# Dealing GpSimd's share of the zero stores to the DMA engines anew, and issuing part of it earlier

## Chip, cores and metric

The kernel runs on one core of one Trainium2 chip. The metric is the device time of one execution in microseconds (us), less is better. Three timed runs gave a median of 272.18 us (272.06 to 272.75). One further execution was recorded by the profiler. TensorE is PE (PEld its weight loads), VectorE DVE, ScalarE ACT, GpSimd POOL and SyncE SP; L302 is line 302 of the kernel before. A queue in which an engine issues its DMAs has a q behind its name (SPq).

## What is computed

The forward is a layer norm, a decode step of grouped-query attention over a sliding window of the cache, a gated feed-forward with GELU, and a residual. The kernel returns its output and the gradients of all inputs for a given `grad_out`. Shapes: batch 4, one token, D = 512, 32 query heads, 8 key/value heads of 128, caches of 4096 positions with a window of the last W = 1024, F = 1792.

```python
def _A_ref(x, k_cache, v_cache, wq, wo):
    q = (x @ wq).reshape(B, Sq, Hq, Dh).transpose(0, 2, 1, 3)
    k = jnp.repeat(k_cache[:, :, Sk - W:, :], rep, axis=1)
    v = jnp.repeat(v_cache[:, :, Sk - W:, :], rep, axis=1)
    scores = jnp.einsum("bhqd,bhkd->bhqk", q, k) * (Dh ** -0.5)
    p = softmax(scores)
    o = jnp.einsum("bhqk,bhkd->bhqd", p, v)
    return o.transpose(0, 2, 1, 3).reshape(B, Sq, Hq * Dh) @ wo

def _B_ref(x, w_gate, w_up, w_down):
    return (gelu(x @ w_gate) * (x @ w_up)) @ w_down

xn = layernorm(x)
out = x + _A_ref(xn, ...) + _B_ref(xn, ...)
# outputs: out, then its gradients to x, k_cache, v_cache, wq, wo, w_gate, w_up, w_down
```

The gradients of the two caches (`out_2`, `out_3`, each 4 x 8 x 4096 x 128 in bf16) are zero in the first K0 = 3072 positions, which lie outside the window. These zeros, 50 MB, are the largest part of what the kernel writes.

## The kernel before

Everything is done once, in stages: layer norm and the feed-forward's forward and backward (matrices `wg_sb`, `wu_sb`, `wd_sb`), the queries (`qr_ps`, `q_ps`), then for each batch entry the attention's forward and backward over the window (tiles `ka`, `kb`, `va`, results through `stg`), at last the weight gradients of `wq` and `wo` (`dw_ps`, tiles `late` and `stg`) and the output rows.

The order of PE, DVE, ACT and POOL instructions is chosen by a scheduler up to the attention loop, from dependences and from the place in the program; there a changed line can move others. SP's order is the written one throughout: it holds all loads and stores but two kinds, and its DMAs run in the order of issue on each DMA engine's queue. An SP instruction that waits holds up all that stand behind it.

**Zeros.** `ztile` (128 partitions of 12288 bytes) is cleared by POOL at L224. A piece is 12288 bytes, 48 positions of one head. `ztodo` lists 32 units, each 2 heads of 64 pieces, 1.5 MB. SP writes 31 of them: `zeros(n)` (L298-307) issues n units, each as one DMA whose source is 64 partitions read twice, and holds each behind the fourth unit before it. `result()` (L114-119) issues as many units ahead of a store as the list `before` says; six more stand behind the loads of `va` and `kb` (L461 and L463: two and four). The 32nd unit (`zog`, `zb`, `zg`: the last of `out_3`) goes by POOL in parts:

```python
    def part_zeros(m0, rows, each, part, after=None):
        z = nc.gpsimd.dma_start(
            out=zog[zb, zg:zg + ZG, 0:K0, :].rearrange("g (m j) d -> m g (j d)", m=ZP)[m0:m0 + rows * each],
            in_=bass.AP(tensor=ztile.tensor, offset=ztile[part:part + 1, :].offset,
                        ap=[[4 * ztile[:].ap[0][0], rows], [0, ZG * each], [1, ZW]]))
```

One call is one DMA: `rows` source partitions (every fourth from `part` on), each read 2 x `each` times. Three calls follow the clearing of `dhs` (L420-424): 3 rows of 10 pieces, 2 rows of 2, 3 rows of 10. A fourth, 8 rows of 8 pieces, stands at the beginning of the last phase (L819) and waits for the last SP unit issued before it.

**The stretch that the prediction walks through** is the feed-forward's backward (L339-391). `a_b` (the product of the two branches) is transposed to `aT` (L346); `aSP`, cleared by POOL at L348, gets four diagonal blocks of `a_b` by four DVE instructions at L350. `wd_sb` is transposed in four parts into `scr` (L94), and 16 matmuls add up `da_ps`; from it DVE makes `dhu` (L373), `ua` (L374, its tile is shown as `stg`) and `dhg` (L375). The 14 matmuls `dwd_ps<-dy_b,aSP` make the gradient of `w_down`; `evac` (L83-92) copies each to `stg` on ACT or DVE, by a running estimate of the load of both. `result()` stores it in two halves, then come the loads of `ka`, and the queries.

Of the kernel before, what the change touches and what calls it, by code (L numbers as in the profile page):

```python
# [19 lines left out]
def kernel(  # L20
# [24 lines left out]
    nc = tc.nc  # L45

    B, Sq, D = A_x.shape
    _, G, Sk, Dh = A_k_cache.shape
# [4 lines left out]
    K0 = Sk - W  # L53
# [29 lines left out]
    def evac(out, in_, n):  # L83

        ca, cd = (190 + n) / 1.2, (130 + n) / 0.96
        eng = "act" if load["act"] + ca <= load["dve"] + cd else "dve"
        load[eng] += ca if eng == "act" else cd
        if eng == "act":
            return nc.scalar.copy(out=out, in_=in_)  # L89
        return nc.vector.tensor_copy(out=out, in_=in_)  # L90

    def t32(out, in_, n):
        load["dve"] += (130 + n) / 0.96
        nc.vector.transpose(out=out, in_=in_)  # L94

    def pairs(ap):
        return ap.bitcast(U32)

    def scratch():
        return scrp.tile([P, 1024], U32, name="scr", tag="scr")  # L100
# [6 lines left out]
    def stg_tile():  # L107

        if not halves:
            pair = stg_pair()  # L110
            halves.extend(pair[:, h] for h in range(2))
        return halves.pop(0)
# [3 lines left out]
    def result(*parts):  # L116
        zeros(min(before.popleft(), len(ztodo)))
        for out, in_ in parts:
            nc.sync.dma_start(out=out, in_=in_)
# [19 lines left out]
    def mm(out, lhsT, rhs, first=True, last=True, pos=None):  # L139
        kw = {} if pos is None else {"tile_position": pos}  # L140
        nc.tensor.matmul(out, lhsT=lhsT, rhs=rhs, start=first, stop=last, **kw)  # L141

    def bank(name, tag="w", shape=(P, 512), dt=FP32):
        pool = {"w": ps_w, "x": ps_x}.get(tag, ps_a)
        return pool.tile(list(shape), dt, name=name, tag=tag)
# [75 lines left out]
    ZP = P // 2  # L221
    ZW = K0 // ZP * Dh
    ztile = const.tile([P, ZW], BF16, name="ztile")
    nc.gpsimd.memset(ztile[:].bitcast(FP32), 0.0)  # L224


    stats = const.tile([P, nc.vector.BN_STATS_DIM], FP32, name="stats")
# [32 lines left out]
    def window(dram, b, h):  # L260

        return dram[b, h * G // 2:(h + 1) * G // 2, K0:Sk, :].rearrange("g (m j) d -> m g (j d)", j=2 * J)

    def alternate(tl, h):

        t_ = tl[h:h + 1]
        return bass.AP(tensor=t_.tensor, offset=t_.offset,
                       ap=[[2 * t_.ap[0][0], P // 2], [2 * J * Dh, G // 2], [1, 2 * J * Dh]])

    def load_kv(b, k, pool, tag, eng, **kw):  # L270
        d_, src = ((k_t, A_k_cache), (v_t, A_v_cache))[k]
        tl = pool.tile([P, G // 2, 2 * J, Dh], BF16, name=tag, tag=tag)
        for h in range(2):
            with tc.high_priority():
                d = eng.dma_start(out=alternate(tl, h), in_=window(src, b, h), **kw)
        d_[b] = tl
        return d

    ZG = 2
    zsrc = bass.AP(tensor=ztile.tensor, offset=ztile.offset, ap=[[2 * ztile[:].ap[0][0], ZP], [0, ZG], [1, ZW]])  # L280
    ztodo = [(og, b, g) for b in range(B) for g in range(0, G, ZG) for og in (out_2, out_3)]
    zdone = []
    zog, zb, zg = ztodo.pop()

    def part_zeros(m0, rows, each, part, after=None):

        z = nc.gpsimd.dma_start(  # L287
            out=zog[zb, zg:zg + ZG, 0:K0, :].rearrange("g (m j) d -> m g (j d)", m=ZP)[m0:m0 + rows * each],
            in_=bass.AP(tensor=ztile.tensor, offset=ztile[part:part + 1, :].offset,
                        ap=[[4 * ztile[:].ap[0][0], rows], [0, ZG * each], [1, ZW]]))  # L290
        if after is not None:
            behind(z.ins, after.ins)

    def behind(ins, other):
        tc.add_manual_dep(ins, other.name,
                          mybir.DependencyInfo(mybir.DependencyClass.Sync, mybir.DependencyReason.DATA))

    def zeros(n, after=None, deep=4):  # L298

        for _ in range(n):  # L300
            og, b, g = ztodo.pop(0)
            z = nc.sync.dma_start(out=og[b, g:g + ZG, 0:K0, :].rearrange("g (m j) d -> m g (j d)", m=ZP), in_=zsrc)  # L302
            if len(zdone) >= deep:
                behind(z.ins, zdone[-deep].ins)
            if after is not None:
                behind(z.ins, after.ins)
            zdone.append(z)


    if True:  # L310
# [5 lines left out]
        def flat(t_):  # L316
            return t_[:].rearrange("p f c -> p (f c)")
# [92 lines left out]
        for wi, (wsb, dh, og) in enumerate(((wu_sb, dhu, out_7), (wg_sb, dhg, out_6))):  # L410
            dh_f = flat(dh)
            dhr = hgu[:].rearrange("p u f c -> p (u f c)").bitcast(BF16)
            for a, q in enumerate(quad):
                ps = bank("rep_ps", "w", (P, FQ))
                mm(ps[:], rsum_b[q, :], dh_f[q, :], pos=(Q * a, 0))
                evac(dhr[:, a * FQ:(a + 1) * FQ], ps[:], FQ)
            dhP = scratch()[:, 0:FPB * Q].rearrange("p (f x) -> p f x", f=FPB)
            t32(dhP, pairs(dhr[:, 0:F]), 896)
            dhs = ffn.tile([P, FPB, 2, 4 * B], BF16, name="dhs", tag=f"dhs{wi}")
            nc.gpsimd.memset(dhs[:], 0.0)  # L420
            if wi == 1:
                part_zeros(0, 3, 5, 0)
                part_zeros(15, 2, 1, 12)
                part_zeros(17, 3, 5, 20)
            dhPb = dhP.bitcast(BF16).rearrange("p f (x r) -> p f r x", r=2)
            for a, q in enumerate(quad):
                nc.vector.tensor_copy(out=dhs[q, :, :, a * B:(a + 1) * B], in_=dhPb[q, :, :, 0:B])
            for ch in range(4):
                sc = scratch()
                n7 = FPB // 4  # L430
                t32(sc[:, 0:n7 * P].rearrange("p (k c n) -> p c k n", k=n7, c=C),
                    pairs(wsb[:])[:, :, ch * n7 * Q:(ch + 1) * n7 * Q], 896)
                sb = sc[:, 0:n7 * P].bitcast(BF16).rearrange("p (k n r) -> p k r n", k=n7, r=2)
                for k in range(n7):
                    c = nm % 4
                    mm(dxf_ps[quad[c]].rearrange("p r n -> p (r n)"), dhs[:, ch * n7 + k].rearrange("p r x -> p (r x)"),
                       sb[:, k], nm < 4, nm >= 2 * FPB - 4, (0, Q * c))
                    nm += 1
            dwg_v = og.rearrange("(p h c) f -> h p (c f)", h=2, c=2)
            for h in range(2):  # L440
                stg = stg_tile()
                for ci in range(2):
                    for a, q in enumerate(quad):
                        ps = bank("dwg_ps", "w", (P, FQ))
                        mm(ps[:], xn_b[q, 2 * h + ci:D:C], dh_f[q, :], pos=(Q * a, 0))
                        o_ = (ci * NQ + a) * FQ
                        evac(stg[:, o_:o_ + FQ], ps[:], FQ)
                result((dwg_v[h], stg[:, 0:2 * F]))
# [4 lines left out]
    with tc.tile_pool(name="mid", bufs=1, reuse_waits="tile") as mid:  # L453
# [4 lines left out]
        with (tc.tile_pool(name="kvp", bufs=1, reuse_waits="tile") as kvp,  # L458
              tc.tile_pool(name="att", bufs=1, reuse_waits="tile") as att):
            load_kv(0, 1, kvp, "va", nc.sync)  # L460
            zeros(2)  # L461
            load_kv(1, 0, kvp, "kb", nc.sync)
            zeros(4)  # L463


# [2 lines left out]
            rows = [qm[:], dyBD[:].rearrange("p n r x -> p (n r x)").rearrange("p (b g d) -> p b g d", b=B, g=4)]  # L468
# [132 lines left out]
            def small(name, shape=(P, 1)):  # L601
                return att.tile(list(shape), FP32, name=name, tag=name)
# [72 lines left out]
            for b in range(B):  # L675
                S = sps[0][:]
                m = small("m")
# [124 lines left out]
            for i in range(KH):  # L802
                t, e, c = i // 8, i // 4 % 2, i % 4
# [12 lines left out]
            s_o = sums[:, 0:D]  # L816
            TT(out=s_o, in0=ob_ps[:], in1=fo[:], op=ALU.add)

            part_zeros(32, 8, 4, 64, zdone[-1])  # L819
            dwo_v = out_5.rearrange("(p t k) n -> t p (k n)", t=4, k=8)  # L820
            dwq_v = out_4.rearrange("(p c) j -> c p j", c=C)
            late = {}
# [126 lines left out]
```

## Time and profile before

| | |
|---|---|
| median of three runs | 272.18 us |
| the profiled execution | 272.15 us |
| its span, first to last instruction | 270.4 us (1.75 us lie around it) |
| busy: PE, PEld, DVE, ACT, POOL | 61%, 23%, 67%, 51%, 13% of the span |
| bytes moved by DMA | 111.90 MB in 16640 packets, mean 414 GB/s |
| SP units of zeros | 31 x 1536 KB, 19.1 us from issue to landing |
| POOL's zeros | 1 x 768 KB (11.9 us to landing), 2 x 360 KB (25.1), 1 x 48 KB (21.9) |
| mean granted TensorE clock | 0.748 |

The page's second part cuts the span into 40 slices; a digit is the busy share in tenths, for DMA the mean over 16 engines. The view of windows gives the same for chosen stretches. A timeline lists one engine's work in order: start, busy time, engine, line, operation, tiles, and in brackets the idle time ahead and what ended it. For SPq the time is that of issuing.

### The profile page before, as it was taken

How to read it: one execution, taken by the hardware profiler on the slowest of the kernel's cores; microseconds unless marked ns; L12 is line 12 of the kernel's file. 1: busy time of each engine (PE TensorE's matmuls, PEld its weight loads, DVE VectorE, ACT ScalarE, POOL GpSimd, SP SyncE). 2: the span in 40 equal slices, each digit the busy share in tenths (PEclk: the TensorE clock that was granted, in tenths of full speed). 3: DMA queues.
4: the chain of work that ended last, by engine and by line, in shares of the span. 5: the costliest groups of instructions: out<-in, count | busy, mean ns of one | idle time of the engine just before them, and what ended most of it. 6: DMA issues, size and time to landing. Idle time of an engine off the chain costs nothing.

```text
span 270.4 us, 3304 instructions
## 1 busy us (share of the span) xinstructions
PE 164.6 (61%) x1152; PEld 62.0 (23%) x1159; DVE 180.5 (67%) x339; ACT 137.4 (51%) x278; POOL 36.1 (13%) x95
## 2 busy tenths in 40 slices
PE   1256988968536687676568578585877898460000
PEld 0121342222112342123222233122421223010000
DVE  7869768978798428873588536793289999970000
ACT  2242775670022636696577765696476666460000
POOL 8900002091032101120012100000000000000000
PEclk9998885556855555997999975997577999555555
DMA  7999999999999999999999999999999999999994
GB/s 264 437 422 449 409 369 425 430 431 413 421 426 428 430 412 425 426 421 427 415 421 418 433 416 421 431 422 431 418 428 425 422 429 417 429 429 428 428 420 207
DMA packets 16640, 111.90 MB, mean 414 GB/s; under 512 B 1760, under 2 KB 1776, under 8 KB 10992
## 3 DMA queue, kind: packets, MB, share of 16 engines
q1 hardware_dynamic: 16072, 110.12, 97.7%
q0 software_dynamic: 544, 1.57, 1.5%
q8 instruction: 9, 0.15, 0.2%
q14 instruction: 7, 0.06, 0.1%
q10 hardware_dynamic: 8, 0.00, 0.0%
HBM read 30.68 MB, written 81.01 MB: 413 GB/s over the span
## 4 chain that ended last, share of the span: by engine, by line
DVE 21%; PE 21%; ACT 17%; issue 4%; ACTq 0%
DVE scr L94 9%; ACT stg L124 6%; ACT spr L584 5%; PE kv_ps L141 4%; PE dw_ps L141 4%; DVE stg L124 3%; PE sc_ps L141 3%; PE ok_ps L141 2%; DVE odt L647 2%; PE od_ps L141 2%; ACT late L124 2%; DVE dqs L763 2%; DVE wq_t L94 2%; PE ob_ps L141 1%; ACT last L124 1%
## 5 line engine op out<-in xcount | busy, mean ns | idle before, releaser
L124 ACT CAST stg<-kv_ps 128x512 bf16<-128x512 f32 x102 | 54.6, 598 | 26.5 <-PE kv_ps L141 26.4
L141 PE MATMUL sc_ps<-scr,bd 128*32 128x256 bf16 x256 | 20.1, 399 | 18.1 <-DVE scr L94 17.5
L141 PEld LDWEIGHTS <-spr 128*128 128x128 bf16 x256 | 17.0, 108 | 36.1 <-issue 24.3
L141 PE MATMUL kv_ps<-dyBD,spr 128*128 128x512 bf16 x60 | 24.1, 528 | 1.9 <-issue 1.3
L141 PE MATMUL kv_ps<-qm,spr 128*128 128x512 bf16 x63 | 19.7, 387 | 3.0 <-DVE stg L124 1.1
L94 DVE STREAM_TRANSPOSE scr<-va 128x1024 uint32<-128x1024 uint32 x16 | 19.5, 1224 | 0.0
L124 DVE CAST stg<-kv_ps 128x512 bf16<-128x512 f32 x10 | 6.6, 688 | 17.9 <-PE kv_ps L141 17.9
L89 ACT CAST stg<-dwg_ps 128x448 bf16<-128x448 f32 x26 | 12.0, 567 | 3.3 <-DMA out_dram<-stg 2.4
L549 POOL COPY bd<-D3q 32x64 bf16<-32x64 bf16 x32 | 7.6, 245 | 44.4 <-PE sc_ps L141 43.2
L141 PEld LDWEIGHTS <-bd 128*32 128x32 bf16 x256 | 6.3, 99 | 29.8 <-issue 27.2
L141 PE MATMUL dw_ps<-scr,xn_b 32*128 32x512 bf16 x32 | 9.4, 545 | 5.5 <-ACT late L124 4.0
L124 ACT CAST late<-dw_ps 128x512 bf16<-128x512 f32 x16 | 9.2, 588 | 6.8 <-PE dw_ps L141 6.7
L141 PE MATMUL do_ps<-scr,dyBD 128*128 128x512 bf16 x31 | 11.1, 491 | 2.3 <-DVE scr L94 1.9
L584 ACT ACTIVATE spr<-dS_b,amask 64x256 bf16<-64x256 bf16 x16 | 7.4, 554 | 8.5 <-DVE dS_b L728 8.5
L549 POOL COPY bd<-D3d 32x64 bf16<-32x64 bf16 x32 | 7.4, 239 | 31.7 <-PE sc_ps L141 16.4
L647 DVE SCALAR_TENSOR_TENSOR odt<-od_ps,om,odt 128x128 f32<-128x128 f32 x12 | 4.2, 351 | 11.1 <-ACT odt L642 10.8
L124 DVE CAST stg<-dw_ps 128x512 bf16<-128x512 f32 x16 | 10.5, 685 | 1.5 <-PE dw_ps L141 1.3
L287 POOL DMA_DIRECT2D out_dram<-ztile x4 | 3.0, 753 | 61.9 <-DMA out_dram<-ztile 61.9
L94 DVE STREAM_TRANSPOSE scr<-wo_sb 128x1024 uint32<-128x1024 uint32 x8 | 9.8, 1237 | 1.6 <-PE do_ps L141 1.0
L124 ACT CAST stg<-dw_ps 128x512 bf16<-128x512 f32 x16 | 8.9, 588 | 3.6 <-PE dw_ps L141 3.4
L94 DVE STREAM_TRANSPOSE scr<-ka 128x1024 uint32<-128x1024 uint32 x8 | 9.8, 1233 | 1.2 <-PE r_ps L141 1.1
L124 DVE CAST late<-dw_ps 128x512 bf16<-128x512 f32 x16 | 10.4, 675 | 0.3 <-PE dw_ps L141 0.3
(203 smaller groups left out, 337.4 us busy)
## 6 DMA issues: line engine op xcount, KB each, us to landing
out_dram<-ztile SPq DMA_DIRECT2D x31, 1536.0 KB, 19.1
out_dram<-stg SPq DMA_DIRECT2D x18, 1024.0 KB, 14.7
va<-in_A_v_cache_dram SPq DMA_DIRECT2D x8, 1024.0 KB, 14.3
out_dram<-stg SPq DMA_DIRECT2D x6, 896.0 KB, 11.9
wq_sb<-in_A_wq_dram SPq DMA_DIRECT2D x1, 4096.0 KB, 27.9
wo_sb<-in_A_wo_dram SPq DMA_DIRECT2D x1, 4096.0 KB, 37.3
ka<-in_A_k_cache_dram SPq DMA_DIRECT2D x4, 1024.0 KB, 15.6
kb<-in_A_k_cache_dram SPq DMA_DIRECT2D x4, 1024.0 KB, 19.0
```

The costliest lines, as they stand in the source:

```text
L89: return nc.scalar.copy(out=out, in_=in_)
L94: nc.vector.transpose(out=out, in_=in_)
L124: return nc.scalar.copy(out=out, in_=in_) if eng == "act" else nc.vector.tensor_copy(out=out, in_=in_)
L141: nc.tensor.matmul(out, lhsT=lhsT, rhs=rhs, start=first, stop=last, **kw)
L287: z = nc.gpsimd.dma_start(out=zog[zb, zg:zg + ZG, 0:K0, :].rearrange("g (m j) d -> m g (j d)", m=ZP)[m0:m0 + rows * each], in_=bass.AP(ten ...
L549: nc.gpsimd.tensor_copy(out=t_[q, :, :, g2, :, o_:o_ + 4], in_=src[q, b, g2])
L584: nc.scalar.activation(out=out, in_=in_, func=ACT.Copy, scale=amask[q, a:a + 1])
L647: STT(out=t_[:], in0=ps[:, g, :], scalar=(om, oms)[k][:, g:g + 1], in1=t_[:], op0=ALU.mult, op1=ALU.add)
L763: nc.vector.tensor_copy(out=dqs[q, :, :, :, a * B + b], in_=d3v[q])
```

## The change

The definitions that belong to the zeros move up to the clearing of `ztile`. There POOL issues two DMAs: 5 rows of 2 pieces and 8 rows of 8. The three calls behind `dhs` go. The call of the last phase has 6 rows of 8 pieces, not 8. The unit's last six pieces (three of each head) go by SP, in one DMA (`rest_zeros`) behind the loads of `kb`; its source is given as 16 rows of 4608 bytes, its destination as 2 x 8 rows. POOL has 3 zero DMAs instead of 4, SP 32 instead of 31; the bytes are the same.

```diff
     nc.gpsimd.memset(ztile[:].bitcast(FP32), 0.0)
+    ZG = 2
+    zsrc = bass.AP(tensor=ztile.tensor, offset=ztile.offset, ap=[[2 * ztile[:].ap[0][0], ZP], [0, ZG], [1, ZW]])
+    ztodo = [(og, b, g) for b in range(B) for g in range(0, G, ZG) for og in (out_2, out_3)]
+    zdone = []
+    zog, zb, zg = ztodo.pop()
+    zpart = zog[zb, zg:zg + ZG, 0:K0, :].rearrange("g (m j) d -> g m (j d)", m=ZP)
...
+    def part_zeros(m0, rows, each, part, after=None):
+
+        z = nc.gpsimd.dma_start(
+            out=zpart[:, m0:m0 + rows * each].rearrange("g m e -> m g e"),
+            in_=bass.AP(tensor=ztile.tensor, offset=ztile[part:part + 1, :].offset,
+                        ap=[[4 * ztile[:].ap[0][0], rows], [0, ZG * each], [1, ZW]]))
+        if after is not None:
+            behind(z.ins, after.ins)
+
+    def rest_zeros(m0):
+
+        n = (ZP - m0) * ZW // 8
+        nc.sync.dma_start(out=zpart[:, m0:ZP].rearrange("g m e -> g (m e)").rearrange("g (k e) -> g k e", k=8),
+                          in_=bass.AP(tensor=ztile.tensor, offset=ztile.offset, ap=[[8 * ztile[:].ap[0][0], 16], [1, n]]))
+
+    part_zeros(0, 5, 1, 0)
+    part_zeros(5, 8, 4, 20)
...
-            if wi == 1:
-                part_zeros(0, 3, 5, 0)
-                part_zeros(15, 2, 1, 12)
-                part_zeros(17, 3, 5, 20)
...
             load_kv(1, 0, kvp, "kb", nc.sync)
+            rest_zeros(61)
             zeros(4)
...
-            part_zeros(32, 8, 4, 64, zdone[-1])
+            part_zeros(37, 6, 4, 52, zdone[-1])
```

More of the change, by code (lines that the diff above doesn't have):

```diff
@@ L224, with behind @@
     nc.gpsimd.memset(ztile[:].bitcast(FP32), 0.0)
+    ZG = 2
[4 more added lines that the diff above has]
+    zpart = zog[zb, zg:zg + ZG, 0:K0, :].rearrange("g (m j) d -> g m (j d)", m=ZP)
+    def behind(ins, other):
+        tc.add_manual_dep(ins, other.name,
+                          mybir.DependencyInfo(mybir.DependencyClass.Sync, mybir.DependencyReason.DATA))
+    def part_zeros(m0, rows, each, part, after=None):
[11 more added lines that the diff above has]
+    part_zeros(5, 8, 4, 20)
     stats = const.tile([P, nc.vector.BN_STATS_DIM], FP32, name="stats")
@@ L277, in load_kv @@
         return d
[L279 to L296, printed above, removed]
     def zeros(n, after=None, deep=4):
```

## The prediction, made before the changed kernel ran

> **What bounds the kernel now.** I read the busy slices of the page first, then the windows by stage, then the queues' and engines' timelines around the moved instructions. On the page:
>
> ```profile
> DMA  7999999999999999999999999999999999999994
> ...
> q1 hardware_dynamic: 16072, 110.12, 97.7%
> q0 software_dynamic: 544, 1.57, 1.5%
> ```
>
> In every slice but the first and the last the DMA engines are nine tenths busy or more, while no compute engine is above 67% of the span. q0 is GpSimd's queue: the 1.57 MB of zeros that the change redistributes. The windows (columns: window, length, PE, PEld, DVE, ACT, POOL, granted clock, DMA share, GB/s):
>
> ```profile
> 30.00:244.00 214.00, 151.51 (x1079) 57.17 (x1083) 157.08 (x285) 126.23 (x261) 24.10 (x76) 0.75 1.01 422
> 244.00:264.00 20.00, 0.00 (x0) 0.00 (x0) 0.00 (x0) 0.00 (x0) 0.00 (x0) 0.50 1.01 426
> 264.00:268.00 4.00, 0.00 (x0) 0.00 (x0) 0.00 (x0) 0.00 (x0) 0.00 (x0) 0.50 0.72 301
> ```
>
> After 244 us nothing computes; the DMA engines drain a backlog. So **the 16 DMA engines are the bound**: a compute delay costs something only if an engine runs out of queued packets, and the time is set by the engine that finishes last. The trace records every DMA packet's start and length; since an engine's next packet starts 3 to 4 ns before the last one's end, they can be laid into 16 chains. None has a gap before its tail. They end at:
>
> - eight engines with eight of GpSimd's 12 KB pieces (all late): 266.5 to 266.9 us, but one of them at 268.88 (it carried two of the nine instruction fetches);
> - six engines with ten pieces (all early): 266.5 to 267.7;
> - two with two pieces: 265.1 and 268.93. The latter's packets are long all through the run, about 5 us in sum.
>
> The end is thus 268.93, the span 270.4, the execution 272.15 (median of the runs 272.18: the same).
>
> **Part 1: who carries the zeros.** Rows went to engines in turn: 3 rows of ten pieces, 2 of two, 3 of ten, then 8 of eight make exactly the counts above. Dealt on, the changed rows give engines 0-2 two early pieces and eight late, 3-4 two, 5-12 eight early, 13-15 eight late. A 12288-byte packet takes 0.457 us. Only 5-7 change their sum (ten to eight, -0.9 us), and they were not last. The two engines at 268.9 keep two and eight pieces. Six pieces move to SP, 16 x 4608 bytes; no such packet is recorded, and between the rows for 4096 (0.155 us) and 7168 bytes (0.268) I take 0.174 each: 0.17 us per engine if all 16 share it, 1.39 us on two if two do. Small DMAs take the lowest engines: x's four rows lie on three chains of ten pieces and one of two, engines 0 to 3. So the two would be 0 and 1, which ended at 267.2 to 267.6 and would end at 268.6 to 269.0. So without delays the last engine stays at 268.9: **0 us**, bounds -0.2 (a piece less beside the slow engine) and +0.2 (one more packet everywhere).
>
> GpSimd issues one DMA less, SP one more. Neither costs anything: the mean GpSimd issue is 0.753 us on an engine that is 13% busy, and one more SP issue (0.3 to 0.9 us in its rows) lies among zeros queued some 19 us ahead of landing.
>
> **Part 2: what the early issue moves.** This decides. GpSimd now:
>
> ```profile
> 5.50 1.89 POOL L247 MEMSET dyBD<- 128x2048 bf16 x1
> 7.33 1.70 POOL L348 MEMSET aSP<- 128x1792 bf16 x1
> 8.98 1.66 POOL L420 MEMSET dhs<- 128x896 bf16 x2
> 10.59 2.35 POOL L287 DMA_DIRECT2D out_dram<-ztile  x3
> ```
>
> In the built changed kernel's order, two DMAs stand between dyBD's memset and aSP's: issue at 7.4 and 8.2 us, and aSP's clearing, 1.6 us later, is still done by 11. But the scheduler then picks another order elsewhere. On VectorE the four aSP instructions go behind dhu, L374 and dhg; on TensorE all sixteen da_ps matmuls now precede the fourteen dwd_ps ones. VectorE, ScalarE and TensorE now:
>
> ```profile
> 17.56 1.11 DVE L94 STREAM_TRANSPOSE scr<-wd_sb 128x896 uint32<-128x896 uint32 x1 [0.84 <-DMA wd_sb<-in_B_w_down_dram]
> ...
> 22.66 2.48 DVE L350 TENSOR_SCALAR aSP<-a_b,gmask 32x448 bf16<-32x448 bf16 x4
> ...
> 27.24 1.10 DVE L94 STREAM_TRANSPOSE scr<-wd_sb 128x896 uint32<-128x896 uint32 x1
> ...
> 30.52 0.68 DVE L373 SCALAR_TENSOR_TENSOR dhu<-da_ps,gmask,gl 128x448 bf16<-128x448 f32 x1 [1.67 <-PE da_ps L141]
> ```
>
> ```profile
> 25.29 0.59 PE L141 MATMUL dwd_ps<-dy_b,aSP 128*128 128x512 bf16 x1 [1.46 <-DVE aSP L350]
> ...
> 29.53 0.95 PE L141 MATMUL da_ps<-scr,dyBD 128*128 128x448 bf16 x4
> ```
>
> Step by step:
> - wd lands later. The first zero packet began 5.15 us after its issue (10.59 to 15.74), so now at 12.5 to 13.4; the wd load's packets (0.53 us each) run to about 15.9. Zero packets alternate with the load's one for one, so on engines 5-12 four or five pieces get in front: 18.1 instead of the 17.54 of the latest engine today, **+0.55**.
> - From that transpose to the last wd transpose's end: 28.34 - 17.56 = 10.78, less 2.48 for aSP = 8.30: 26.4. Four da matmuls, 0.95: dhu at 27.45. dhu, L374 and dhg (0.68, 0.68, 0.62, slightly overlapped): aSP at 29.4, done at 31.9. The first dwd matmul follows 0.15 us later (25.14 to 25.29 today): 32.05, **+6.8**.
> - The first store of dwd is issued at 29.91, 4.6 us after that matmul. The eight da matmuls no longer interrupt the fourteen; I take 4.2 to 4.6: 36.3 to 36.7, **+6.5**. On SP the second store and the two ka loads queue behind it.
> - Some comes back:
>
> ```profile
> 43.34 1.41 ACT L89 CAST stg<-dwg_ps 128x448 bf16<-128x448 f32 x3 [2.40 <-DMA out_dram<-stg]
> ```
>
> ScalarE waits 2.40 us for the first store to free its buffer. That store lands hardly later than now on the slowest engines, so with everything later this wait can vanish. After it compute stays busy on itself to 244, so the rest remains: a delay D between 6.5 - 2.4 = 4.1 and 6.5; I take **5.0**, as that buffer's next wait may take part of it again.
>
> **Part 3: do the DMA engines run dry?** SP's issues:
>
> ```profile
> 29.91 4.03 SPq L119 DMA_DIRECT2D out_dram<-stg  x2
> 33.98 1.59 SPq L275 DMA_DIRECT2D ka<-in_A_k_cache_dram  x2
> ...
> 172.44 1.37 SPq L119 DMA_DIRECT2D out_dram<-stg  x2
> ```
>
> From issue to the first packet on the engine that gets there first: 5.87 us for the first store (29.91 to 35.78), 3.5 at 59.07, 2.14 at 172.44. It needs 1.04 (the first load: 0.81 to 1.85). So the slack over that need is 4.8, 2.4 and 1.1 us. An engine that lags behind the first by n pieces has 0.46n more. Eight early pieces (5-12) give 3.7 us more and never run dry. Engines 13-15 have none: dry for 6.5 - 4.8 = 1.7 us at 36, for 5.0 - 2.4 = 2.6 in all by 59 us, 5.0 - 1.1 = **3.9** in all by 172. They end at 266.5 to 266.9 + 3.9 = 270.4 to 270.8. Engines 0-2 (two pieces, 0.9 of lag): 267.2 to 267.6 + 3.0, or + 1.7 + 1.39 for two of them = 270.2 to 270.7. Together **270.6**, where now 268.93 is last: +1.7.
>
> **Sum.** 272.15 + 0 + 1.7 = **273.8 us** (+0.6%). Of D, 3.1 us costs nothing, since engines 13-15 have 2.0 to spare besides the 1.1. With D = 4.1 the end is 269.9 (273.1), with D = 6.5 it is 272.3 (275.5).
>
> **Rivals.**
> 1. Hidden: the delay shrinks below 3.1 us, or the backlog covers it. For: no engine runs dry today, and the 2.40 wait shows that compute has room. Against: 6.5 is over twice 3.1. 271.9 to 272.5.
> 2. Two engines carry SP's rest. A row first: x, four rows, ran on four engines, the 64- and 128-row transfers on 16. The destination here is 2 x 8 x 2304, the source 16 rows; if both slowest counts decide, it goes to two engines. With a small D (0.8 us dry) they end at 267.2 to 267.6 + 1.39 + 0.8 = 269.4 to 269.8: 272.6 to 273.0. [...]
> 3. Slower still: nothing is regained (D = 6.5: 275.5), or the engine that ended at 268.88 is among 13-15 and adds 3.9 to that: 272.8, so 276.0. It decides from D = 1.1 for that engine. Which number it has, the records don't show; three of eight.
> 4. Faster: the two engines at 268.9 are late because of GpSimd's late pieces or their descriptors, and the last phase now has six rows. Then the end is that of the others, 267.7: 271.0. Against: the slow engine's packets are long from the beginning, and it had two pieces only.
>
> **Chances.** Forecast (273.0 to 274.8) 0.50, hidden 0.15, two engines 0.08, slower still 0.17, faster 0.10. A difference of 0.3% (0.8 us) is about what a measurement of this kernel can tell from no change; half of the second rival lies beyond it: slower 0.71, same 0.19, faster 0.10. The range 272.0 to 275.4 leaves out the faster case and the far end of the third rival.
>
> **What would show it.** The aSP group starts near 29.4 instead of 22.66; the first store's issue near 36.5 instead of 29.91, the one of 172.44 some 5 us later; gaps of the DMA engines at 36 to 65 us; the tail beyond 244 us still full, ended 1 to 3 us later. I am wrong if the SP issues stand within 3 us of their old places, or if the DMA share has no gap and the time rises all the same.

## The result, and the profile after

| | before | changed |
|---|---|---|
| median | 272.12 us (272.01 to 272.75) | 280.34 us (280.09 to 282.0) |
| ratio | | 1.031 (95%: 1.028 to 1.034) |
| span of the profiled execution | 270.4 us | 278.4 us |
| last DMA engine done, by its chain of packets | 268.93 us | 277.16 us |

The change costs 8.2 us, 3.1%. Slower was forecast, but 273.8 us, and 275.4 as the upper end. The page after the change:

```profile
DMA  7999969999999999999999999999999999999994
...
q1 hardware_dynamic: 16090, 110.19, 96.9%
q0 software_dynamic: 336, 1.50, 1.3%
```

There is now a 6 in the row of nines: the sixth slice, 34.8 to 41.8 us. The windows (the three shown of before, and two from that slice; columns as before):

```profile
30.00:244.00 214.00, 149.67 (x1076) 55.64 (x1084) 156.23 (x285) 126.33 (x264) 24.25 (x76) 0.77 1.00 407
244.00:264.00 20.00, 2.43 (x8) 0.44 (x7) 3.24 (x6) 2.82 (x5) 0.00 (x0) 0.50 1.01 426
264.00:268.00 4.00, 0.00 (x0) 0.00 (x0) 0.00 (x0) 0.00 (x0) 0.00 (x0) 0.50 1.01 423
...
36.00:38.00 2.00, 2.00 (x7) 0.65 (x5) 0.00 (x0) 2.00 (x5) 0.00 (x0) 0.50 0.42 180
38.00:40.00 2.00, 1.89 (x10) 0.46 (x12) 0.96 (x2) 2.00 (x5) 0.00 (x0) 0.84 0.66 280
```

The last two windows in the kernel before:

```profile
36.00:38.00 2.00, 1.30 (x11) 0.74 (x11) 1.26 (x3) 1.27 (x4) 0.00 (x0) 1.00 0.89 364
38.00:40.00 2.00, 1.81 (x5) 0.47 (x5) 1.99 (x4) 2.00 (x6) 0.00 (x0) 0.66 1.06 447
```

From 36 to 40 us the DMA engines of the changed kernel are about half idle; this is called the dry stretch. And in the long first window the share is 1.00 as before, but the rate is 407 GB/s instead of 422: the engines are as busy and move less, so packets have become longer. Both have to be explained.

Where the stretch was moved, by the timelines of GpSimd, VectorE and SP's queue:

```profile
7.32 1.38 POOL L238 DMA_DIRECT2D out_dram<-ztile  x2
8.69 1.60 POOL L357 MEMSET aSP<- 128x1792 bf16 x1
10.22 1.65 POOL L429 MEMSET dhs<- 128x896 bf16 x2
```

```profile
7.52 4.38 DVE L219 CAST selr<-rs 128x32 bf16<-128x32 f32 x1
...
20.37 1.11 DVE L94 STREAM_TRANSPOSE scr<-wd_sb 128x896 uint32<-128x896 uint32 x1 [1.53 <-DMA wd_sb<-in_B_w_down_dram]
...
29.64 0.68 DVE L382 SCALAR_TENSOR_TENSOR dhu<-da_ps,gmask,gl 128x448 bf16<-128x448 f32 x1 [0.54 <-PE da_ps L141]
...
31.50 2.50 DVE L359 TENSOR_SCALAR aSP<-a_b,gmask 32x448 bf16<-32x448 bf16 x4
```

```profile
38.31 2.79 SPq L119 DMA_DIRECT2D out_dram<-stg  x2
41.15 2.52 SPq L303 DMA_DIRECT2D ka<-in_A_k_cache_dram  x2
...
178.57 1.69 SPq L119 DMA_DIRECT2D out_dram<-stg  x2
```

aSP starts 8.84 us later (31.50 for 22.66), the first store is issued 8.40 later (38.31 for 29.91), the one of 172.44 6.1 later. `selr` of VectorE, 1.53 us before, lasts until GpSimd has cleared `dhs` (11.90 and 11.87).

**Long packets.** A measure used from here on: for each DMA packet of SP's and GpSimd's queues, its time above the usual one of its size (0.159 us for 4096 bytes, 0.272 for 7168, 0.535 for 14336, 0.460 for 12288, the median for the other sizes), summed and divided by 16 engines. It is called the excess. It is 2.69 us per engine in the kernel before and 8.33 in the changed one. The two largest parts of the growth of 5.6 us lie in two places: the stores and loads after the dry stretch (60 to 80 us: 2.11 for 0.17), and the time of the late GpSimd rows (210 to 240 us: 1.43 for 0.18), where 34 of SP's 12288-byte packets take over 800 ns; in the kernel before none does. These two make 3.2 us of it; smaller parts lie at 40 to 50 us (0.86), and near 15, 85 and 145 us (0.4 to 0.6 each).

### The profile page after: what moved, and what is told of

Read it like the earlier page. It is cut to its first block, busy times and chain, and to the rows that moved or that the text cites. A ratio compares the mean times of both kernels' runs of the same rounds, so it can differ in the third digit from the quotient of the medians.

```text
span 278.4 us, 3304 instructions
## 1 busy us (share of the span) xinstructions
PE 162.7 (58%) x1152; PEld 59.8 (21%) x1159; DVE 182.9 (66%) x339; ACT 136.6 (49%) x278; POOL 35.2 (13%) x94
## 4 chain that ended last, share of the span: by engine, by line
PE 26%; DVE 22%; ACT 18%; DMA 17%; issue 5%; SPq 1%; DVEq 0%; ACTq 0%
DMA out_dram<-ztile 8%; DVE scr L94 7%; DMA wd_sb<-in_B_w_down_dram 6%; ACT stg L124 6%; PE kv_ps L141 4%; ACT spr L590 4%; PE dw_ps L141 4%; PE dwg_ps L141 3%; DVE stg L124 3%; DMA va<-in_A_v_cache_dram 3%; ACT stg L89 2%; DVE dqs L769 2%; PE sc_ps L141 2%; DVE odt L653 2%; ACT late L124 2%
## 5 line engine op out<-in xcount | busy, mean ns | idle before, releaser
L141 PE MATMUL kv_ps<-dyBD,spr 128*128 128x512 bf16 x60 | 23.0, 500 | 1.9 <-issue 1.3
L141 PE MATMUL kv_ps<-qm,spr 128*128 128x512 bf16 x63 | 20.9, 413 | 2.2 <-DVE stg L124 1.1
L89 ACT CAST stg<-dwg_ps 128x448 bf16<-128x448 f32 x26 | 11.9, 574 | 1.9 <-PE dwg_ps L141 1.8
L141 PE MATMUL do_ps<-scr,dyBD 128*128 128x512 bf16 x31 | 9.5, 426 | 2.7 <-DVE scr L94 1.7
L94 DVE STREAM_TRANSPOSE scr<-kb 128x1024 uint32<-128x1024 uint32 x8 | 9.9, 1240 | 0.1
```

## The experiments

The first four take the parts of the change apart. Times are medians; ratios go with the kernel before on the same chip, which took 272.2 to 272.6 us in these comparisons.

**e1_old_place**: the changed kernel with its two early DMAs at the old place; aSP's order is then the old one.

```diff
-    part_zeros(0, 5, 1, 0)
-    part_zeros(5, 8, 4, 20)
...
             if wi == 1:
+                part_zeros(0, 5, 1, 0)
+                part_zeros(5, 8, 4, 20)
```

> The changed kernel with its two early DMAs put back behind the clearing of dhs: new dealing of the pieces, six late rows and SP's rest stay, and the instruction order of PE, DVE and ACT is that of the kernel before. Theory A (the early issue delays the first stores, the DMA engines run dry, all else follows): the first store is issued near 29.9 us again, no dry DMA window, 272.0 to 273.0 us. Theory B (the new dealing costs: SP's packets beside the six late rows take 0.34 us longer, 2.6 us per engine, and SP's rest adds 1.4 us on two engines): 274.5 us or more with the first store at 29.9.

275.57 us, ratio 1.008 (1.005 to 1.011). First store at 29.18, no dry slice, yet slower, as the second theory had it: the dealing alone costs 2 to 3 us. The excess from 210 to 240 us is 1.78 us per engine.

**e2_old_split_early**: the old three calls and the old late call (8 rows), but the early ones behind `ztile`'s clearing.

> The kernel before with its own dealing (3 rows of 10, 2 of 2, 3 of 10, late 8 of 8, nothing on SP), the three early DMAs issued right behind ztile's clearing. PE and DVE order is that of the changed kernel. Theory A: first store near 38 us and 277 to 281 us. Theory B: 272 to 273 us although the store is late.

280.96 us, 1.025 (1.017 to 1.032); first store at 40.07, first transpose of wd at 21.47. The place alone costs most of it: 6.8 us by the ratio, with the old dealing. `selr` takes 0.18 us here (VectorE's stall falls on a copy of `dyBD` instead, 3.63 us from 9.22 on), and the transpose still waits 2.78 us for wd's load; so it is the load, not the stall of VectorE, that comes late.

**e7_order_alone**: the kernel before, the four aSP instructions written behind dhg; no zeros moved.

```diff
         nc.gpsimd.memset(aSP[:], 0.0)
-        for q in quad:
-            TS(out=aSP[q, :, q], in0=a_b[q].rearrange("p f c -> p c f"), scalar1=gmask[q, 0:1], scalar2=None,
-               op0=ALU.mult)
...
         TT(out=dhg[:], in0=ua[:], in1=gp[:], op=ALU.mult)
+        for q in quad:
+            TS(out=aSP[q, :, q], in0=a_b[q].rearrange("p f c -> p c f"), scalar1=gmask[q, 0:1], scalar2=None,
+               op0=ALU.mult)
```

> The kernel before, the four instructions that make aSP's blocks written behind dhg: no zero DMA is moved, aSP comes after dhu (two of the four interleaved with L374 and dhg), all da_ps matmuls before dwd_ps. Only the order is tested. Theory A: the first store is 3 to 5 us late (33 to 35), engines stay fed at 36 us, 272.2 to 274 us; so the order alone is under a third of the loss. Rival (the order is the whole delay): first store at 36 or later, 276 us or more.

```profile
35.28 2.79 SPq L119 DMA_DIRECT2D out_dram<-stg  x2
```

274.88 us, 1.007 (1.004 to 1.010); first store 5.4 us late. Both lie between what the two theories gave. The order costs by itself, with an excess of 1.63 us per engine from 60 to 80 us, although no zero packet moved.

**e4_rest16**: the changed kernel, SP's rest as two DMAs of 16 rows of 2304 bytes, meant for 16 engines instead of two.

> The changed kernel, SP's rest as two DMAs of 16 rows of 2304 bytes (one per head), so that all 16 engines share it. If the two engines that carry it end last because of it, 278.9 to 279.4 us; if it lies beside other losses, 280.0 to 280.6.

280.32 us, 1.026 (1.022 to 1.031); no gain beyond the intervals. **e9_old_place_rest16**, the same on e1:

> As e1_old_place, but SP writes its six pieces as two DMAs of 16 rows of 2304 bytes, so that they can be shared by 16 engines; in e1 two engines carried all of it, 8 packets of 178 ns each. Theory 'the two engines with the rest end last': 0.8 to 1.4 us below e1's 275.57 (274.2 to 274.8). Rival 'the rest costs nothing of its own': the same as e1 within 0.4 us.

275.85, 1.011 (1.006 to 1.015), as e1. In the changed kernel the rest is 16 packets of 178 ns, 8 on each of two chains, as the prediction's second rival had it; but these two engines alone don't set the time.

### The late rows

**e8_late_spread**: e1, late rows from partitions 20 apart.

```diff
-            part_zeros(37, 6, 4, 52, zdone[-1])
+            part_zeros(37, 6, 4, 4, zdone[-1], apart=20)
```

> The new dealing with the two early DMAs at their old place (as e1_old_place), but the six late rows are read from partitions 4, 24, 44, 64, 84, 104 of the zero tile instead of 52, 56, ... 72. Theory: in e1 the zero packets of other engines took about 950 ns instead of 460 between 218 and 226 us because several DMA engines read the same neighbouring partitions at once; then that excess is gone here and the time is 1.5 to 2.7 us below e1's 275.57 (272.9 to 274.1). Rival: the excess has another reason (the number of late pieces, the queue): the long packets stay and the time is 275 to 276.

275.83 us, 1.010 (1.006 to 1.015), excess 1.53: that the partitions are neighbours is not the reason.

**e12_late_aligned** (on e1) and **e13_halves** (on the kernel before) change where in the output the rows are written; the early rows, and in e12 SP's rest, move to the pieces that this leaves. Of each only the late call is shown:

```diff
-            part_zeros(37, 6, 4, 52, zdone[-1])
+            part_zeros(52, 3, 4, 52, zdone[-1])
+            part_zeros(0, 3, 4, 64, zdone[-1])
```

```diff
-            part_zeros(32, 8, 4, 64, zdone[-1])
+            part_zeros(0, 8, 4, 64, zdone[-1])
```

> As e1_old_place, but each late row of GpSimd goes to the pieces with the numbers that the same engine writes in SP's units: rows 52 to 63 and 0 to 11 of the unit instead of 37 to 60 (two DMAs of 3 rows instead of one of 6). Theory: in e1 and in the changed kernel the late zeros of one engine and SP's zeros of another are written at the same offset within a head (1 MB apart) at the same time, and so six engines' packets took twice as long between 218 and 226 us; then the long packets are gone and the time falls by 1.5 to 2.7 us from e1's 275.57 to 272.9 to 274.1. Rival: they come from the six rows or the engines that carry them; then the same as e1.

> The kernel before with the two halves of GpSimd's unit exchanged: pieces 32 to 63 go early and 0 to 31 late; engines, counts and places in the program stay. Theory of the same offset: the eight late rows now collide with SP's zeros of the eight other engines, the packets near 220 us grow long as in e1, and the time rises by 1.5 to 3 us to 273.7 to 275.5. Rival (rows and engines): within 0.3% of the kernel before.

e12: 275.73 us, 1.010 (1.007 to 1.014), excess 1.96. e13: 272.24 us, 0.998 (0.996 to 1.001), excess 0.30. Both results contradict the theory (its premise on which pieces an engine writes in SP's zeros was an assumption that no record shows); the output's place doesn't matter. What e13 and the kernel before share against e1, e8 and e12 is the source of the rows. That gave a new theory, tried from both sides, each with little more than one number changed. In the kernel before, GpSimd's 16 rows, dealt in turn, are read from every fourth partition: 0 to 28 for engines 0 to 7, 64 to 92 for engines 8 to 15. The partition of an engine's row there is called its group here; a row read from any other is called foreign.

**e16_late_own**: e1, each late row from the group of the engine that carries it.

```diff
-            part_zeros(37, 6, 4, 52, zdone[-1])
+            part_zeros(37, 3, 4, 84, zdone[-1])
+            part_zeros(49, 3, 4, 0, zdone[-1])
```

> As e1_old_place, but the late rows are read from other partitions of the zero tile: 84, 88, 92 for engines 13 to 15 and 0, 4, 8 for engines 0 to 2 (52 to 72 in e1), in two DMAs of 3 rows. [...] Here every late row reads its own engine's group: the excess between 210 and 230 us falls from some 1.5 us per engine to below 0.3, and the time by 1.5 to 2.7 us to 272.9 to 274.1. Rival 'six rows as such': excess and time as in e1.

**e17_late_other**: the kernel before, late rows from the groups of other engines.

```diff
-            part_zeros(32, 8, 4, 64, zdone[-1])
+            part_zeros(32, 8, 4, 0, zdone[-1])
```

> The kernel before with one number changed: the eight late rows, carried by engines 8 to 15, are read from partitions 0 to 28 instead of 64 to 92, the groups of engines 0 to 7. Theory 'shared ports': packets of engines 0 to 7 take twice as long while they last, 2 to 3.5 us on each; these engines ended at 265 to 267.7, so the end is 270 to 271 and the time 273.2 to 275, with an excess of 1 us or more per engine between 210 and 230 us. Rival: the source does not matter, within 0.3% of the kernel before and no excess.

The window of 218 to 226 us, in turn of before, e1, e16 and e17 (last two columns: DMA share and GB/s):

```profile
218.00:226.00 8.00, 7.55 (x79) 2.29 (x78) 7.05 (x13) 5.15 (x10) 0.00 (x0) 1.00 0.99 415
```

```profile
218.00:226.00 8.00, 7.47 (x63) 1.44 (x60) 5.44 (x9) 4.00 (x7) 0.00 (x0) 0.50 0.99 342
```

```profile
218.00:226.00 8.00, 7.58 (x82) 2.59 (x74) 7.08 (x12) 5.21 (x10) 0.00 (x0) 1.00 1.01 416
```

```profile
218.00:226.00 8.00, 7.81 (x60) 2.04 (x59) 5.58 (x10) 4.00 (x7) 0.00 (x0) 0.50 1.00 315
```

With the engines equally busy, 342 GB/s become 416 when the rows read their own groups, and 415 become 315 when they read foreign ones. e16: 272.95 us, 1.000 (0.997 to 1.003), excess 0.20. e17: 275.73 us, 1.012 (1.005 to 1.020), excess 2.25, of which some two thirds lie in SP's packets and one third in GpSimd's own. So **the source partitions are the cause**, worth 2.6 us by the medians (275.57 to 272.95) and 2.1 by the ratios. In e1 the two chains that end last (272.85 and 271.10 us) are slowed ones, with 4.0 and 3.2 us of this excess. Over all kernels, more than 20 of SP's zero packets above 800 ns are found from 210 to 240 us in those whose late rows read foreign groups, and at most one in the others. The early rows on engines 8 to 12 are still foreign in e16, and cost nothing there that the time shows. Which engine has which number is inferred from the order of dealing; the records don't name it.

In e1 and the changed kernel, each with six foreign late rows, six chains without late pieces were slowed, in the changed kernel by 2.6 to 3.6 us each. Why a foreign row slows another engine's packets is not shown: no record has the partition that an engine reads in SP's zeros, and the ports in the theory's name appear in no run.

### The delay and the long packets

**e10_delay_b** (22 of these, e11: 12), the kernel before with its zeros as they were:

```diff
         TT(out=a_b[:], in0=gl[:], in1=hu[:], op=ALU.mult)
+        for _ in range(22):
+            TS(out=a_b[:], in0=a_b[:], scalar1=1.0, scalar2=None, op0=ALU.mult)
```

> The kernel before with its zeros untouched, and 22 multiplications of a_b by 1.0 in place on VectorE ahead of aSP, some 8 us of added delay there. Theory 'the delay of the stores alone makes most of the loss': first store issued at 37 to 39 us and 277 to 280 us in all. Rival 'the new dealing and the early zeros make the loss': the delay finds some 4 us of cover and the time stays at 275 or below.

> As e10_delay_b with 12 multiplications, some 4 to 5 us of delay. Theory 'the loss grows with the delay past a cover of a few us': 273 to 275 us with the first store at 34 to 35 us. Rival: within 0.3% of the kernel before.

e10, the page and SP's queue:

```profile
DMA  7999939999999999999999999999999999999993
```

```profile
40.80 2.79 SPq L119 DMA_DIRECT2D out_dram<-stg  x2
```

SP's queue in e11:

```profile
36.62 2.79 SPq L119 DMA_DIRECT2D out_dram<-stg  x2
```

283.67 us, 1.041 (1.034 to 1.047); the changed kernel's dry slice is there, deeper, with no change to the zeros. e11: 276.87 us, 1.016 (1.009 to 1.022). Each time was above its range (by 3.7 and 1.9 us); the stores also came later than meant. With e7, delays of 5.4, 6.7 and 10.9 us cost 1.9, 4.2 and 11.0 us (ratio times 272.4): about 1.6 to 1.8 us for each, and by extension of that line nothing up to some 4 us. The changed kernel's 8.4 us lie at 7.0 on this line (an estimate). It is a rough one, for e2, whose rows read their own groups too, has a delay of 10.2 us and costs 6.8 (4.8 to 8.8), some 3 us less than the line gives. **The delay is the larger cause.** It costs more than the dry time because the packets behind the dry stretch are long: 60 to 80 us, 2.09 in e10, 1.66 in e11.

Why they are long was tried in two ways. **e14_all_late**: the three early calls moved behind the late one, so no engine has early pieces. **e15_delay_stagger**: e11 with these calls waiting for dhg, which puts eight engines behind again.

> The kernel before with its three early GpSimd DMAs moved behind the late one, so that no engine has early pieces and all 16 are equally far in their queues from the start, with the stores issued as early as before. Theory 'in step': engines that are equally far in their queues make each other's packets long; then the loads of va and kb (60 to 80 us) have an excess near 1 us per engine, as in the delayed kernels (0.15 in the kernel before). Rival 'short backlog': packets grow long where their DMA is issued only shortly before it starts; then the excess between 60 and 80 us stays near 0.2. The time is of less use, since the end carries more zeros: 272 to 275 by either.

> e11_delay_a with the three early GpSimd DMAs held until dhg is done, so that eight of the engines fall behind the others again after the dry window. Theory 'in step': with the engines out of step as in the kernel before, the excess of the loads between 60 and 80 us falls from e11's 1.66 us per engine to 0.5 or less, and the time to 274 to 276. Rival 'short backlog': the eight engines without these pieces keep their long packets, at least 0.8 us per engine in the mean, and the time is 276 to 278, since the zeros that covered part of the wait came too late.

e14 has 0.46 from 60 to 80 us, far from 1; e15 has 1.65 like e11: being in step is not the cause. (e14 took 279.87 us, far above its range: with nothing dealt ahead, its eight late rows fell on engines 0 to 7, and the early ones on 8 to 15, all foreign, with 4.20 us of excess. e15: 275.75, 1.013 from 1.007 to 1.020.)

**e20_unit_first**: the changed kernel, one SP unit of zeros moved from the last phase to ahead of the first store.

```diff
-    before = deque([0, 0, 0, 1, 1, 1] + [0, 2] + [0, 2] + [0, 3] + [3, 2] + [1] * 5 + [0] * 3)
+    before = deque([1, 0, 0, 1, 1, 1] + [0, 2] + [0, 2] + [0, 3] + [3, 2] + [1] * 4 + [0] * 4)
```

> The changed kernel with one unit of SP's zeros taken from the last phase and issued ahead of the first store of dwd, so that every DMA engine has 3.7 us more to do while the store is awaited; nothing else moves. Theory 'dry engines and the long packets that follow': the dry stretch at 36 to 40 us goes, and with it most of the excess of the second store and of the loads of ka and va; 275 to 277. Rival 'the long packets come from elsewhere': only the 3.8 us of dry time goes on engines that had it, the packets stay long, and the time is 278 or more.

277.63 us, 1.019 (1.013 to 1.026), between the two expectations, although the first store stays at 37.91. Its windows:

```profile
36.00:38.00 2.00, 2.00 (x7) 0.64 (x5) 0.00 (x0) 2.00 (x5) 0.00 (x0) 0.50 0.78 307
38.00:40.00 2.00, 1.89 (x13) 0.54 (x15) 1.36 (x2) 2.00 (x5) 0.00 (x0) 0.93 0.92 392
```

The share is back at 0.78 and 0.92, and the excess of the first stores' and ka's packets falls from 0.89 us per engine to 0.12. The later loads keep theirs (60 to 80 us: 1.41). **e21_zeros_ahead**: e11 with two units of zeros ahead of va's loads.

> e11_delay_a (the kernel before with a pure delay of the first stores) with two lines exchanged: SP issues the two units of zeros that stood behind the loads of va ahead of them, so that va's loads find 7 us of queued work. Theory 'short queue': loads have long packets only where little is queued ahead of them; the excess between 60 and 80 us falls from e11's 1.66 us per engine to below 0.5, and the time by 1 us or more to 275 to 276, if va's later landing holds up nothing. Rival 'after a dry stretch the engines stay disturbed, whatever is queued': the excess stays above 1 us and the time at 276.5 or more.

276.83 us, 1.016 (1.011 to 1.022), as e11. From 60 to 80 us the excess falls to 0.66, but 0.79 appears from 80 to 90: it moved to the last packets of the zeros ahead of va (0.42 at 74 to 76 us) and to the end of kb (0.62 at 84 to 86 us). Neither expectation on the excess holds: it is not the depth of the queue alone. Why these packets are long remains open.

**e3_behind_asp**: the changed kernel, the two early DMAs one instruction further down.

```diff
-    part_zeros(0, 5, 1, 0)
-    part_zeros(5, 8, 4, 20)
...
         nc.gpsimd.memset(aSP[:], 0.0)
+        part_zeros(0, 5, 1, 0)
+        part_zeros(5, 8, 4, 20)
```

> The changed kernel with its two early DMAs one instruction further down on GpSimd, behind aSP's clearing instead of ahead of it; the scheduler then leaves the four aSP instructions where the kernel before has them. Theory 'the late stores make most of the loss': first store near 30 to 32, hardly any dry time, and the time of e1_old_place, 275 to 276.5. Rival 'the early issue itself' (the load of wd and VectorE held up): the store stays beyond 33 and the time at 277.5 or more.

```profile
23.42 2.49 DVE L359 TENSOR_SCALAR aSP<-a_b,gmask 32x448 bf16<-32x448 bf16 x4
```

276.9 us, 1.015 (1.010 to 1.020), just above the first theory's range; first store at 30.23. 3.4 us come back by where one line stands. What is left goes with the foreign late rows (excess 1.53), and with va's loads, issued at 62.67 (59.50 before): here the scheduler places dhs's copies behind a copy that waits 4.40 us for the first store's buffer, at 47.74 and 56.25 (39.50 and 49.45 before). How much each is worth was not measured.

**e22_three_mended**: e3, all rows from their own groups, and e20's unit first.

> The changed kernel with its three faults mended: the early DMAs behind aSP's clearing (as e3), every GpSimd row read from the group of partitions of the engine that carries it, early ones too (as e16 did for the late ones), and one unit of SP's zeros ahead of the first store (as e20). Theory: these three, the late stores, the foreign partitions and the short queue behind them, are the whole loss, so the time is within 0.5% of the kernel before, 271.5 to 273.5. Rival: something of the early issue costs by itself; 274 or more.

280.17 us, 1.028 (1.025 to 1.031), far outside the theory's 271.5 to 273.5. The excess from 210 to 240 us is gone (0.12), but the page shows an 8 and a 6, and VectorE and SP's queue show waits:

```profile
DMA  7999999999899996999999999999999999999993
```

```profile
47.09 0.62 DVE L90 CAST stg<-dwg_ps 128x448 bf16<-128x448 f32 x1 [6.31 <-DMA out_dram<-stg]
56.41 0.62 DVE L90 CAST stg<-dwg_ps 128x448 bf16<-128x448 f32 x1 [5.43 <-DMA out_dram<-stg]
```

```profile
59.09 0.34 SPq L119 DMA_DIRECT2D out_dram<-stg  x1
69.36 1.80 SPq L301 DMA_DIRECT2D va<-in_A_v_cache_dram  x2
```

The first wait is e3's of 4.40, now 6.31; the second, 5.43, is new. With the stores early again, the unit ahead of them makes them land later, VectorE waits for their buffers, and va's loads go out 10 us late (3 in e3). What covered the delay in e20 is a delay here, on top of e3's changed order. So no version here beats the kernel before, and that the two causes are the whole loss wasn't shown by mending them.

## Why the prediction was wrong in size

- **The bound** held: the end is that of the DMA engines, 277.16 us.
- **Part 1, "0 us", failed.** It counted pieces per engine and never asked which partitions a row reads. Without the delay, as Part 1 asks, that is worth 2.6 us (e1 against e16), and its bounds of 0.2 had no room for it. The rest by SP was sized right: 8 x 178 ns = 1.42 us on two engines, for 1.39.
- **Part 2, wd +0.55: mis-sized, it is +2.81** (20.37 for 17.56). The first zero packet began at 11.89 us, ahead of 12.5, and 60 zero packets began before the load's last one ended (6 before), 50 of them on the eight engines, some six on each, not four or five; 53 of the 256 packets of the two loads of 14336-byte rows (`wu` and `wd`) took over 600 ns (7 before). The next step, aSP behind dhg, was right: the 8.84 us are 6.8 and 2.04 more, about the 2.26 by which wd was missed. The first store then is +8.40 for +6.5, and D is 6.1 for 5.0.
- **Part 3, the dry time, came out in its sum, in part by luck**: engines 13 to 15 have gaps of 4.3 us, for 3.9; but 3.8 of it lies at 35 us, where 1.7 was forecast, and little comes later. Its slack of 4.8 us at the first store holds: 8.4 - 4.8 = 3.6. Engines 0 to 4 have 1.9 to 2.8 us, those with eight early pieces none there. **What failed is the step from there to the end**, which left every packet at its old duration. On the mean engine they grew by 5.6 us.
- **Which engines end last.** The chains can be followed by the gaps between packets and the order of sizes in SP's DMAs; where chains stand level, some ends can be exchanged. The four that end at 276.8 to 277.2 us all carry late pieces and have at most 0.3 us of excess from 210 to 240 us. The six that the foreign rows slow, by 2.6 to 3.6 us, end at 274.1 to 275.0. So the 1.25 us by which this time's excess grew on the mean engine is not on the last chains: 266.5 to 266.9 + 4.3 + 4.4 = 275.2 to 275.6 for engines 13 to 15, and 1 to 2 us of the last ends stay unaccounted for.
- **Rivals.** The nearest was "slower still", 275.5 with D = 6.5 (276.0 by its other branch); it too was priced at one for one, where e7, e11 and e10 show some 1.6 for one past the cover. "Two engines" was there as a mechanism, but not in the time. "Hidden" and "faster" are excluded by a loss of 8.2 us.

So two causes are shown, each by itself: the late stores (6.8 us in e2; about 7.0 by the line through e7, e11 and e10) and the foreign partitions (about 2.6 where the stores are on time). They don't add up to 9.6 in the changed kernel, for there the slowed engines end some 2 us before the last; what the foreign rows add to its 8.2 us was not measured, since no run mends them alone there. That the delay costs dry time and long packets is shown; what makes these packets long is not.

## What to carry over

A transfer is dealt to DMA engines and to partitions at once: when pieces go to other engines, the partitions they read from have to go with them (2.6 us here, e1 against e16). An instruction put ahead on an engine can turn a scheduler's order somewhere else, so the order of every engine is to be read, and the delay priced with what lies behind the dry stretch. A cover ahead of a late transfer helped here only as long as the transfer was late (e20: 277.63 us for the changed kernel's 280.34; e22: 280.17 for e3's 276.9). A loss that is shown by itself can lie on engines that don't end last, so follow the one that does.

## What the runs showed of the chip beyond that

- A 12288-byte packet of zeros takes 0.46 us. Where late rows are foreign, both sides pay: in e17, while the late rows move (218.6 to 226.3 us), SP's packets take 663 ns in the mean (the 40 slowest 0.81 to 0.97 us) and GpSimd's 628, for 464 and 461 before.
- Behind the dry stretch, packets at the end of loads that zeros or stores follow were long: va's second load in the changed kernel has an excess of 1.29 us per engine, in the kernel before 0.15.
- VectorE's `selr`, statistics and transpose stood until 11.9 us beside GpSimd's DMA issue and clearings, up to 4.38 us. `selr` lasts from 7.52 to 11.90, over GpSimd's issue and its clearings of aSP and dhs, the last of which ends at 11.87; why the two ends lie together is not shown. The transpose of wd still waited 1.53 us for its load afterwards, so the stall was not the last thing in its way.
